# Moving one w2 row between partition halves, starting two programs on a new fetch block, and shortening the VectorE program in a decode kernel

## The chip, the cores and the metric

The kernel runs on one core of one Trainium2 chip. The time is the device time of that core in microseconds (us). The medians here come from 3 to 9 runs, and an interval is a 95% interval over fast runs. The core's executions agree within about 0.15%. The span on a profile page (399.3 us before) is about 1.3 us shorter than the timed run it belongs to (400.63 us).

Words used below. A *DMA engine* is one of the 16 that the page counts for the core. A *completion* is one engine's count on a load's semaphore: a 128-partition load has 16 of them here, and the trace has the time of each. A DMA of 8 partitions has eight. The eight engines on which these run are called *lower*, the other eight *upper*. The recorded texts write 0-7 or "the eight lowest" for the lower and 8-15 for the upper ones. These numbers are labels only: no trace numbers the engines.

## The reference

One token of attention with a cache (32 query heads, 4 key/value heads, 65,536 positions, head size 128) plus a small MLP, on the same normalised input:

```python
x  = A_x                                   # [1, 1, 1024], bf16
xn = layernorm(x)
out = x + A(xn, k_cache, v_cache, wq, wo) + B(xn, w1, w2, w3, w4)

def B(x, w1, w2, w3, w4):                  # w1, w2 1024x1024; w3 1024x3584; w4 3584x1024
    h  = gelu(layernorm(x) @ w1)
    hs = concatenate(shifted quarters of h) @ w2   # one position: every shifted quarter is zero
    x1 = x + hs
    return x1 + gelu(layernorm(x1) @ w3) @ w4
```

The caches are 67 MB each, and about 170 MB are read in all. Because there is one position, the vector that meets w2 is zero. The kernel still loads and multiplies w2.

## The kernel before

Everything large goes through three slots of 8 MB in on-chip memory, loaded by 128-partition DMAs from SP. The prologue loads wq, w1 and w2, and w3. The middle alternates K and V blocks. The end loads wo and then w4 in four parts. The parts that matter here, with cuts marked:

```python
# w2: rows 8p .. 8p+7 on partition p (in the trace 128 packets of 16 KiB; each engine takes 4.89 to 4.92 us)
kv_load(1, "w1", rows_src(B_w1, 0, 8), 8 * D, b_w1)
_dma(q_sp, chan("w2"), lambda e: e.dma_start(out=KV[:, 1, 8 * D:16 * D], in_=rows_src(B_w2, 0, 8)), writes=b_w2)
kv_load(2, "s2", rows_src(B_w3, 0, 8), 8 * F)
# ... cut ...
for h in range(HKV):                       # 16 small mask products
    for we in range(4):
        _op(q_dve, ... tensor_tensor(out=Yall[:, h, we, :, :], ...))
# ... cut: per group of the softmax, but for the first of a head ...
_op(q_dve, ... tensor_tensor(out=dd[:, k:k + 1], in0=brun[:, k:k + 1], in1=brun[:, o:o + 1], op=ALU.subtract))
_op(q_act, ... activation(ff[:, k:k + 1], dd[:, k:k + 1], ACTF.Exp))
# ... cut: the end ...
w4_parts = [(0, 17), (17, 7), (24, 3), (27, 1)]      # four loads; the last is 256 KB
# PE multiplies each part as it lands; DVE copies the result; SP stores it
# ... cut: SP and ACT issue their first load ahead of the start barrier ...
heads = {e: next(i for i in code if i.opcode == "Drain" and i.engine == e) for e in (nc.sync.engine, nc.scalar.engine)}
```

## Time and profile before

| | |
|---|---|
| time, median of 3 | 400.3 us (400.18 to 400.79) |
| read from HBM | 169.87 MB |
| instruction fetches in the span | five of 16 KiB, two of 8 KiB |
| last load complete | 396.78 us |

Three lines of the page: each engine's busy time, the DMA engines' busy tenths in 40 slices, and the shares by engine of the chain of work that ended last.

```profile
PE 177.8 (45%) x1539; PEld 61.1 (15%) x1539; DVE 221.3 (55%) x260; ACT 23.9 (6%) x50; POOL 7.7 (2%) x31
...
DMA  9999899999999999999999999999999999999995
...
DMA 58%; DVE 25%; PE 14%; issue 1%; ACT 1%; SPq 1%; POOL 0%
```

No compute engine is near full. The DMA engines are busy 90% or more in every slice but the fifth (80% or more) and the last. The 25% of DVE in the chain is not time lost: it is mostly the transposes of line 460 (17%), behind which SP issues a later load. A load issued late does no harm here while the queue ahead of it is still full: the K load issued at 71.52 us stands behind one that completes at 86.92 to 89.22.

The DMA queues (packets, MB, share of 16 engines' time), from the same page:

```profile
q1 hardware_dynamic: 3608, 169.87, 98.7%
q8 instruction: 5, 0.08, 0.1%
q10 hardware_dynamic: 144, 0.00, 0.0%
q14 instruction: 2, 0.02, 0.0%
```

Queue 1 is the kernel's loads. Queues 8 and 14 fetch the engines' programs (the page's kind "instruction"). They are under a thousandth of the bytes (0.10 of 169.97 MB).

The end of the chain, in order of time (start, length, what):

```profile
363.85 32.93 DMA KV<-in_B_w_dram
396.78 0.04 issue
396.82 0.31 PE S_ps L566 x4
397.13 0.02 issue
397.16 0.42 DVE orow L647
```

The kernel ends when the last w4 load is complete on its slowest DMA engine (396.78), plus a fixed tail of about 2.5 us. The 16 completions of this load, read from the semaphore's records in the trace:

```
394.48 394.58 394.65 394.67 394.70 394.71 394.74 394.77 394.85 394.93 394.98
396.08 396.16 396.46 396.51 396.78
```

Eleven engines are done within 0.5 us, and five come 1.1 to 1.8 us after the eleventh. The trace's packets show why. A full 64 KiB packet takes 2.418 us. After a 16 KiB fetch (at 46.4, 81.6, 103.9 and 142.3 us) one engine has a gap of about 1.0 us and then a packet slower by 0.5 us, about 1.55 us together, each time another engine. After the 8 KiB fetches (55.0 and 259.3 us) one engine loses 0.31 + 0.66 = 0.97 us, both times the same one. What an engine has lost it does not regain. The engine that ends the w3 load last (50.48 us) is 2.17 us behind the fifth of that load, and at the end the last is 2.08 us behind the fifth (396.78 against 394.70). In the first load the next packet of an engine starts 2 ns after the last one ends (95 of the 96 packets that start between 4 and 18 us), which leaves nothing to catch up in. That this holds for the later loads too would explain it, and fits the full slices. The fifth 16 KiB fetch, at 394.38 us, adds no late engine: the same number, five, is late in the loads before it.

The groups of instructions that write `Yall` and `dd` (line, engine, operation, count: ns min/median/max, first and last start):

```profile
L395 DVE TENSOR_TENSOR Yall<-M_ps,KV x16: 191/191/191, 36.0 to 39.4; 128x32 bf16<-128x32 f32 x16
...
L500 DVE TENSOR_TENSOR dd<-brun x12: 158/159/160, 95.1 to 364.9; 128x1 f32<-128x1 f32 x12
```

### The profile page before, as it was taken

Reading aid. Unit: us, or ns where it says so; the run is one execution under the profiler, and the core shown is the slowest. Engines: PE = TensorE matmul, PEld = TensorE weight load, DVE = VectorE, ACT = ScalarE, POOL = GpSimd, SP = SyncE. Lnnn points to the kernel's source line nnn. Section 1 sums busy time; section 2 is a strip of 40 time slices with the busy share of each in tenths; the row PEclk is TensorE's granted clock in tenths of the full one; section 3 lists DMA queues with packets and bytes.
Section 4 is the critical chain, followed back from the end, with each engine's and each line's share of the span. In section 5 each row is a group of like instructions: output and inputs, shape, how many; then the busy total and the mean of one; then the engine's idle time right before and its main releaser. Section 6 shows DMA issues by size and latency. Waiting matters only on the chain.

```text
span 399.3 us, 3500 instructions
## 1 busy us (share of the span) xinstructions
PE 177.8 (45%) x1539; PEld 61.1 (15%) x1539; DVE 221.3 (55%) x260; ACT 23.9 (6%) x50; POOL 7.7 (2%) x31
## 2 busy tenths in 40 slices
PE   0035669147134713560358036413661462147394
PEld 0022435012001110110012001100120110012232
DVE  0024230995298539843984597269647952895201
ACT  1000000011001100110011002000100110011000
POOL 5000000000000000000000000000000000000000
PEclk9998656555755665585557555855565558555979
DMA  9999899999999999999999999999999999999995
GB/s 420 420 387 487 382 441 479 440 415 427 415 427 427 433 474 433 420 427 420 433 427 433 473 433 420 421 420 433 433 433 473 433 420 420 420 433 433 416 424 219
DMA packets 3759, 169.97 MB, mean 426 GB/s; under 512 B 548, under 2 KB 552, under 8 KB 808
## 3 DMA queue, kind: packets, MB, share of 16 engines
q1 hardware_dynamic: 3608, 169.87, 98.7%
q8 instruction: 5, 0.08, 0.1%
q10 hardware_dynamic: 144, 0.00, 0.0%
q14 instruction: 2, 0.02, 0.0%
HBM read 169.87 MB, written 0.00 MB: 425 GB/s over the span
## 4 chain that ended last, share of the span: by engine, by line
DMA 58%; DVE 25%; PE 14%; issue 1%; ACT 1%; SPq 1%; POOL 0%
DMA KV<-in_A_k_cache_dram 44%; DVE KV L460 17%; DMA KV<-in_B_w_dram 8%; DMA KV<-in_A_x_dram 6%; PE S_ps L411 3%; PE OT_ps L518 3%; DVE mrow L481 2%; PE M_ps L426 2%; PE S_ps L474 2%; PE S_ps L379 2%; ACT p_sb L496 1%; DVE Yall L395 1%; PE PT_ps L505 1%; DVE pT_f L509 1%; DVE pT_f L419 1%
## 5 line engine op out<-in xcount | busy, mean ns | idle before, releaser
L460 DVE STREAM_TRANSPOSE KV<-KV 128x4096 f32<-128x4096 f32 x32 | 140.3, 4421 | 42.2 <-DMA KV<-in_A_k_cache_dram 42.2
L474 PE MATMUL S_ps<-KV,Ycur 128*32 128x512 bf16 x512 | 60.7, 623 | 126.1 <-DVE KV L460 126.1
L518 PE MATMUL OT_ps<-KV,pT_f 128*32 128x512 bf16 x512 | 46.6, 504 | 1.2 <-DVE pT_f L509 1.2
L474 PEld LDWEIGHTS S_ps<-KV,Ycur 128*32 128x32 bf16 x512 | 14.3, 126 | 158.1 <-DVE KV L460 140.5
L496 ACT ACTIVATE p_sb<-S_ps,brun 128x1024 bf16<-128x1024 f32 x16 | 17.8, 1114 | 274.7 <-DVE brun L494 174.3
L509 DVE STREAM_TRANSPOSE pT_f<-PT_ps 128x512 f32<-128x512 f32 x32 | 22.4, 701 | 14.0 <-PE PT_ps L505 14.0
L481 DVE TENSOR_REDUCE mrow<-S_ps 128x1 f32<-128x1024 f32 x16 | 19.3, 1204 | 11.3 <-PE S_ps L474 11.3
L484 PE MATMUL M_ps<-Rm,Lmat 128*128 128x16 bf16 x16 | 3.1, 194 | 38.0 <-DVE Rm L482 38.0
L505 PE MATMUL PT_ps<-p_sb,permR 128*128 128x512 bf16 x32 | 18.3, 573 | 0.8
L529 DVE SCALAR_TENSOR_TENSOR O_acc<-O_acc,ff,OT_ps 128x512 f32<-128x512 f32 x12 | 9.0, 747 | 14.4 <-PE OT_ps L518 14.4
L518 PEld LDWEIGHTS OT_ps<-KV,pT_f 128*32 128x32 bf16 x512 | 12.9, 114 | 23.6 <-issue 15.5
L411 PE MATMUL S_ps<-KV 128*32 128x512 bf16 x88 | 12.5, 571 | 2.7 <-DVE KV L359 2.7
L339 DVE CAST KV<-KV 128x8 f32<-128x8 bf16 x1 | 0.2, 172 | 22.4 <-DMA KV<-in_A_x_dram 22.4
L578 PE MATMUL S_ps<-KV,o_bf 128*1 128x512 bf16 x64 | 9.7, 476 | 4.8 <-DMA KV<-in_A_wo_dram 4.8
L484 PEld LDWEIGHTS M_ps<-Rm,Lmat 128*128 128x128 bf16 x16 | 1.7, 104 | 49.3 <-DVE Rm L482 49.3
L426 PE MATMUL M_ps<-ident_f,pT_f 64*128 64x2 f32 (+2 forms) x32 | 7.9, 372 | 2.4 <-DVE pT_f L419 2.4
L582 DVE COPY pT_f<-S_ps 1x512 f32<-1x512 f32 x1 | 0.7, 679 | 14.4 <-PE S_ps L578 14.4
L426 PEld LDWEIGHTS M_ps<-ident_f,pT_f 64*128 64x128 f32 (+2 forms) x32 | 7.7, 326 | 4.7 <-DVE pT_f L419 3.4
L419 DVE COPY pT_f<-S_ps 64x512 f32<-64x512 f32 (+1 forms) x3 | 2.1, 685 | 11.3 <-PE S_ps L411 11.3
L505 PEld LDWEIGHTS PT_ps<-p_sb,permR 128*128 128x128 bf16 x32 | 3.3, 102 | 27.2 <-ACT p_sb L496 14.7
L364 PE MATMUL M_ps<-KV 8*128 8x8 bf16 x1 | 0.2, 182 | 16.2 <-DVE Dmat_f L363 16.2
L379 PE MATMUL S_ps<-KV 128*32 128x512 bf16 x64 | 6.5, 593 | 1.4 <-DVE KV L359 1.4
(88 smaller groups left out, 88.8 us busy)
## 6 DMA issues: line engine op xcount, KB each, us to landing
KV<-in_B_w_dram SPq DMA_DIRECT2D x1, 7168.0 KB, 48.4
KV<-in_B_w_dram SPq DMA_DIRECT2D x1, 4352.0 KB, 27.4
KV<-in_B_w_dram SPq DMA_DIRECT2D x2, 2048.0 KB, 28.4
KV<-in_B_w_dram SPq DMA_DIRECT2D x1, 1792.0 KB, 31.4
KV<-in_B_w_dram SPq DMA_DIRECT2D x1, 768.0 KB, 32.8
KV<-in_B_w_dram SPq DMA_DIRECT2D x1, 256.0 KB, 32.9
KV<-in_A_k_cache_dram SPq DMA_DIRECT2D x8, 46.5
KV<-in_A_v_cache_dram SPq DMA_DIRECT2D x8, 28.0
```

Source lines behind the costliest of these rows:

```text
L379: fns.append(lambda e, j=j, b=b, jj=jj: e.matmul(S_ps[32 * jj:32 * jj + 32, b, :], xn_bf[:, j:j + 1].broadcast_to([P, 32]), KV[:, 0, j * H ...
L411: fns.append(lambda e, j=j, k=k, mv=mv: e.matmul(S_ps[32 * (k % 4):32 * (k % 4) + 32, bank + k // 4, :], vec[:, j:j + 1].broadcast_to([P, ...
L426: fns.append(lambda e, b=b, nb=nb, c=c: e.matmul(M_ps[:, c0 + 16 * b + c:c0 + 16 * b + 4 * nb:4], pT_f[0:32 * nb, b, c:512:4], ident_f[0:3 ...
L460: _op(q_dve, lambda e: e.transpose(out=KV32[:, s, o:o + 4096], in_=KV32[:, s, o:o + 4096]), reads=[b_KV[s][sub]], writes=[b_KV[s][sub]], l ...
L474: fns.append(lambda e, we=we, cm=cm, mv=mv: e.matmul(S_ps[32 * cm:32 * cm + 32, n % 4, :], Ycur[:, we, :, :].rearrange("p a g -> p (a g)") ...
L481: _op(q_dve, lambda e: e.reduce_max(mrow[:, k:k + 1], S_ps[:, 2 * k:2 * k + 2, :].rearrange("p b c -> p (b c)"), axis=AX.X), reads=b_S[2 * ...
L496: _op(q_act, lambda e: e.activation(p_sb[:, :, :].rearrange("p b c -> p (b c)"), S_ps[:, 2 * k:2 * k + 2, :].rearrange("p b c -> p (b c)") ...
L505: _op(q_pe, lambda e: e.matmul(PT_ps[:, :], permR[:, :], p_sb[:, n % 2, :], start=True, stop=True), reads=[b_p[n % 2], b_const], writes=[b ...
L509: _op(q_dve, lambda e: e.transpose(out=pT_f[:, n % 2, :], in_=PT_ps[:, :]), reads=[b_PT], writes=[b_pT[n % 2]], loop=True)
L518: fns.append(lambda e, q=q, q4=q4: e.matmul(OT_ps[32 * q4:32 * q4 + 32, g % 2, :], pT_bf[:, n % 2, q, :, 1], KV[:, s, 8192 * sub + 512 * q ...
L529: _op(q_dve, lambda e: e.scalar_tensor_tensor(out=O_acc[:, 0:512], in0=O_acc[:, 0:512], scalar=ff[:, k:k + 1], in1=OT_ps[:, k, :], op0=ALU ...
L578: _grp(q_pe, [lambda e, j=j, jj=jj: e.matmul(S_ps[32 * jj:32 * jj + 1, 1, :], o_bf[:, j:j + 1], KV[:, 0, j * D + 512 * jj:j * D + 512 * (j ...
```

## The change

Its intent, as I read it from its code: let the engines that end early carry more of w2, save instruction fetches by starting PE's and VectorE's programs on a block boundary, and shorten the VectorE program. The diff, cut to its core:

```diff
-_dma(q_sp, chan("w2"), lambda e: e.dma_start(out=KV[:, 1, 8 * D:16 * D], in_=rows_src(B_w2, 0, 8)), writes=b_w2)
+NLO = 2
+NALL = KT_D - NLO // 2                    # seven rows on every partition ...
+_dma(q_sp, chan("w2"), lambda e: e.dma_start(out=KV[:, 1, 8 * D:(8 + NALL) * D], in_=B_w2[0:P * NALL, :]...), writes=b_w2)
+for i in range(8):                        # ... and two more on partitions 0-63, by 8 DMAs of 8 partitions
+    hf, c = divmod(i, 4)
+    p0 = 32 * hf + c
+    _dma(q_sp, chan("w2%d" % i), lambda e, ...: e.dma_start(out=KV[p0:32 * (p0 // 32) + 32:4, 1, ...], in_=src), writes=[b_w2x[i]])
 ...
-for h in range(HKV):
-    for we in range(4):                   # 16 products of 32 columns
+for we in range(4):                       # 4 products of 128 columns
 ...
-_op(q_dve, ... tensor_tensor(out=dd[:, k:k + 1], in0=brun[:, k:k + 1], in1=brun[:, o:o + 1], op=ALU.subtract))
-_op(q_act, ... activation(ff[:, k:k + 1], dd[:, k:k + 1], ACTF.Exp))
+_op(q_act, ... activation(ff[:, k:k + 1], brun[:, o:o + 1], ACTF.Exp, bias=brun[:, k:k + 1], scale=-1.0))
 ...
+for eng, slots in ((nc.tensor, 256), (nc.vector, 128)):
+    eng.addr_align(slots, offset=0, max_nops=0)   # in the trace: a new branch on each, at 0.31 us (PE) and 0.09 us (VectorE)
+    # ... moved in front of the engine's first instruction
```

The w2 product gets two more matmuls, on the two extra rows of partitions 0-63 alone (also in the diff; cut here).

More of the change, by code (lines that the diff above doesn't have):

```diff
@@ L205, in bass_parallel_sum__gqa_block_cached__mixer_s_mlp__decode_kernel @@
         brun = sb("brun", [P, 2], F32)
-        dd = sb("dd", [P, 2], F32)
         ff = sb("ff", [P, 2], F32)
@@ L254, in bass_parallel_sum__gqa_block_cached__mixer_s_mlp__decode_kernel @@
         qT_bf = early(HQ, BF)
-        g_bf = early(KT_D, BF)
+        g_bf = early(2 * KT_D, BF)
         h1g_bf = early(KT_D, BF)
@@ L285, in bass_parallel_sum__gqa_block_cached__mixer_s_mlp__decode_kernel @@
         b_p = [_B(), _B()]; b_pT = [_B(), _B()]
-        b_mrow = [_B(), _B()]; b_R = [_B(), _B()]; b_B = [_B(), _B()]; b_brun = [_B(), _B()]; b_dd = [_B(), _B()]; b_ff = [_B(), _B()]; b_lp = [_B(), _B()]
+        b_mrow = [_B(), _B()]; b_R = [_B(), _B()]; b_B = [_B(), _B()]; b_brun = [_B(), _B()]; b_ff = [_B(), _B()]; b_lp = [_B(), _B()]
         b_Oacc = _B(); b_L = _B(); b_cb = _B(); b_cbW = _B(); b_Mc = _B(); b_o = _B(); b_orow = _B()
@@ L299, in bass_parallel_sum__gqa_block_cached__mixer_s_mlp__decode_kernel @@
         kv_load(1, "w1", rows_src(B_w1, 0, 8), 8 * D, b_w1)
-        _dma(q_sp, chan("w2"), lambda e: e.dma_start(out=KV[:, 1, 8 * D:16 * D], in_=rows_src(B_w2, 0, 8)), writes=b_w2)
+        NLO = 2
+        NALL = KT_D - NLO // 2
+        b_w2x = [_B() for _ in range(8)]
+        _dma(q_sp, chan("w2"), lambda e: e.dma_start(out=KV[:, 1, 8 * D:(8 + NALL) * D], in_=B_w2[0:P * NALL, :].rearrange("(p r) n -> p (r n)", p=P)), writes=b_w2)
+        for i in range(8):
+            hf, c = divmod(i, 4)
+            p0 = 32 * hf + c
+            src = bass.AP(B_w2.tensor, B_w2.offset + (P * NALL + p0 * NLO) * D, [[4 * NLO * D, 8], [1, NLO * D]])
+            _dma(q_sp, chan("w2%d" % i), lambda e, p0=p0, src=src: e.dma_start(out=KV[p0:32 * (p0 // 32) + 32:4, 1, (8 + NALL) * D:(8 + NALL + NLO) * D], in_=src), writes=[b_w2x[i]])
         kv_load(2, "s2", rows_src(B_w3, 0, 8), 8 * F)
@@ L392, in bass_parallel_sum__gqa_block_cached__mixer_s_mlp__decode_kernel @@
                     for we in range(4)], reads=[b_qT, b_const], writes=[b_M])
-        for h in range(HKV):
-            for we in range(4):
-                _op(q_dve, lambda e, h=h, we=we: e.tensor_tensor(out=Yall[:, h, we, :, :],
-                                                                 in0=M_ps[:, 128 + 32 * we + 8 * h:128 + 32 * we + 8 * h + 8].unsqueeze(1).broadcast_to([P, 4, G]),
-                                                                 in1=maskA, op=ALU.mult),
-                    reads=[b_M, b_const], writes=[b_Y], partial=(h + we > 0))
+        for we in range(4):
+            _op(q_dve, lambda e, we=we: e.tensor_tensor(out=Yall[:, :, we, :, :],
+                                                        in0=M_ps[:, 128 + 32 * we:128 + 32 * we + HQ].rearrange("p (h g) -> p h g", g=G).unsqueeze(2).broadcast_to([P, HKV, 4, G]),
+                                                        in1=maskA.unsqueeze(1).broadcast_to([P, HKV, 4, G]), op=ALU.mult),
+                reads=[b_M, b_const], writes=[b_Y], partial=(we > 0))
         _op(q_dve, lambda e: e.tensor_tensor(out=acc[:], in0=xT, in1=xn, op=ALU.add), reads=[b_xT, b_xn], writes=[b_acc])
@@ L402, in bass_parallel_sum__gqa_block_cached__mixer_s_mlp__decode_kernel, with proj @@
         kvstep = KV[:].ap[0][0]
-        def proj(s, o, ncol, vec, bank, reads, c0):
+        def proj(s, o, ncol, vec, bank, reads, c0, nlow=0):
             nper = ncol // P
@@ L407, in proj @@
             fns = []
-            for j in range(KT_D):
+            njs = KT_D + nlow // 2
+            for j in range(njs):
+                pp = P if j < njs - nlow else P // 2
                 for k in range(nt):
-                    mv = bass.AP(KV[:].tensor, s * SLOT + o + j * ncol + 4 * k, [[kvstep, P], [nper, P], [1, 4]])
-                    fns.append(lambda e, j=j, k=k, mv=mv: e.matmul(
-                        S_ps[32 * (k % 4):32 * (k % 4) + 32, bank + k // 4, :], vec[:, j:j + 1].broadcast_to([P, 32]), mv,
-                        start=(j == 0), stop=(j == KT_D - 1), tile_position=(0, 32 * (k % 4))))
+                    mv = bass.AP(KV[:].tensor, s * SLOT + o + j * ncol + 4 * k, [[kvstep, pp], [nper, P], [1, 4]])
+                    fns.append(lambda e, j=j, k=k, mv=mv, pp=pp: e.matmul(
+                        S_ps[32 * (k % 4):32 * (k % 4) + 32, bank + k // 4, :], vec[0:pp, j:j + 1].broadcast_to([pp, 32]), mv,
+                        start=(j == 0), stop=(j == njs - 1), tile_position=(0, 32 * (k % 4))))
             nbank = (nt + 3) // 4
@@ L442, in bass_parallel_sum__gqa_block_cached__mixer_s_mlp__decode_kernel @@
         gelu(M_ps[:, 256:256 + KT_D], KT_D, h1g_bf, b_M, b_h1)
-        proj(1, 8 * D, D, g_bf, 3, b_w2 + [b_const], 272)
+        proj(1, 8 * D, D, g_bf, 3, b_w2 + b_w2x + [b_const], 272, NLO)
         _op(q_dve, lambda e: e.tensor_tensor(out=x1, in0=xn, in1=M_ps[:, 272:272 + KT_D], op=ALU.add), reads=[b_xn, b_M], writes=[b_x1])
@@ L499, in EXP @@
             if not first:
-                _op(q_dve, lambda e: e.tensor_tensor(out=dd[:, k:k + 1], in0=brun[:, k:k + 1], in1=brun[:, o:o + 1], op=ALU.subtract),
-                    reads=[b_brun[o], b_brun[k]], writes=[b_dd[k]])
-                _op(q_act, lambda e: e.activation(ff[:, k:k + 1], dd[:, k:k + 1], ACTF.Exp), reads=[b_dd[k]], writes=[b_ff[k]])
+                _op(q_act, lambda e: e.activation(ff[:, k:k + 1], brun[:, o:o + 1], ACTF.Exp, bias=brun[:, k:k + 1], scale=-1.0), reads=[b_brun[o], b_brun[k]], writes=[b_ff[k]])
         def PT(n):
@@ L651, in bass_parallel_sum__gqa_block_cached__mixer_s_mlp__decode_kernel @@
         code = nc.m.functions[0].blocks[0].instructions
-        heads = {e: next(i for i in code if i.opcode == "Drain" and i.engine == e) for e in (nc.sync.engine, nc.scalar.engine)}
+        heads = {e: next(i for i in code if i.opcode == "Drain" and i.engine == e) for e in (nc.sync.engine, nc.scalar.engine, nc.tensor.engine, nc.vector.engine)}
+        for eng, slots in ((nc.tensor, 256), (nc.vector, 128)):
+            eng.addr_align(slots, offset=0, max_nops=0)
+            align = code[-1]
+            assert align.engine == eng.engine
+            code.remove(align)
+            code.insert(code.index(heads[eng.engine]), align)
         n_before = len(code)
```

## The prediction

> **What bounds the kernel.** The DMA engines. The page's slices show DMA at 9 tenths everywhere, 169.97 MB at 426 GB/s, and the chain of waits gives DMA 58%. A full 64 KiB packet takes 2.418 us in the trace, so one of 16 engines needs about 391.7 us for its share of 10.6 MB (estimate from those two); the span is 399.3. The compute engines have slack: DVE is busy 55%, PE 45%, and every load is issued 15 us or more before the queue ahead of it runs dry (DMA issues: the K load issued at 71.5 us follows one that lands at 87-89). So removed VectorE and prologue work is worth about nothing by itself.
>
> What ends last: the 16 engines' completions of the last w4 load. Eleven come at 394.48-394.98 us, five at 396.08-396.78; then 0.3 us PE, 0.4 us DVE, 1.6 us output DMA. The five late engines were delayed by instruction fetches: the DMA queue view lists "instruction" packets, five of 16 KiB (46, 82, 104, 142, 394 us) and two of 8 KiB (55, 259 us). Each of the first four is followed by a gap of about 1.0 us and a 0.55 us slower packet on one engine, each time another one: about 1.55 us. The two 8 KiB ones cost about 0.97 us each, on the same fifth engine. [...]
>
> **What the change does.**
> 1. w2: [...] Nine rows against seven moves 16 KiB per engine: 0.60 us (2.418/4) from each upper to each lower engine. It helps only if the late engines are the upper ones; the trace doesn't number engines, so this is inferred from the change's intent. Eight small DMAs add perhaps 0.03-0.05 us each on the lower engines (estimate from what is left of the 393 us after the packets), 8 issues of about 0.4-0.7 us on SP and 8 waits of 51 ns on PE, all in slack.
> 2. Alignment and fewer VectorE instructions (12 mask products and 14 subtractions, of 271): the VectorE program fits two 128-instruction blocks, so of its fetches at 55 and 259 us one remains, near 160 us: 0.97 us less on one engine. PE still crosses about as many blocks, so I expect three to five 16 KiB fetches at shifted times, still about 1.5 us each on different engines. Both programs jump at the start; what that fetches falls at about time zero, and could cost one engine another 1.5 us.
> 3. 26 VectorE operations of about 0.16-0.2 us: about 5 us of busy time, off the path.
>
> **Sum.** Late upper engines end at about 396.8 - 0.6 = 396.2; lower engines at about 395.0 + 0.6 + 0.3 = 395.9. The tail is unchanged. Gain about 0.6 us: 399.7 us, 80% range 398.9 to 400.5. Faster by over 2%: 0.005; within 2%: 0.985; slower by over 2%: 0.01.
>
> **What would show it.** The last load's completions in a tighter band: earliest about 395, last about 396.1. VectorE instruction packets 2 to 1 in the span; PE ones 5 to 4-5. DVE busy about 216 us. Same HBM bytes.
>
> **What would make it wrong.** Late engines in the lower half (then 0.6 us slower). A PE fetch near the end, or two PE fetches on one engine (about 1.5 us more). More gain (over 1 us) if alignment takes PE fetches out of the loading time or spreads them. A start-up delay from the jumps, if the timer includes it.

The sum: 396.8 - 0.6 = 396.2 us for the late upper engines, 395.0 + 0.6 + 0.3 = 395.9 us for the lower ones, and so a gain of 0.6 us and 399.7 us. The 0.6 is a quarter of the 2.418 us of a 64 KiB packet.

## The result, and the profile after

401.21 us (401.12 to 401.32, 6 runs) against 400.39 us (400.18 to 400.79, 6 runs of before): slower by 0.8 us. The ratio is 1.0019, interval [1.0006, 1.0032]. Every ratio in this document is the mean time of one kernel's fast runs over that of the other's fast runs of the same rounds, so not quite the ratio of the quoted medians. By the 2% measure this is "the same". It is a loss all the same, because the ranges don't touch, and the prediction had a gain.

The lines of the page after that answer to those above:

```profile
PE 176.2 (44%) x1541; PEld 60.2 (15%) x1541; DVE 217.6 (54%) x236; ACT 25.0 (6%) x50; POOL 7.6 (2%) x31
...
q1 hardware_dynamic: 3736, 169.87, 98.6%
q8 instruction: 6, 0.10, 0.1%
...
q14 instruction: 2, 0.02, 0.0%
```

VectorE has 24 operations fewer and is busy 3.7 us less (foreseen: 26 and about 5 us). But there are six 16 KiB fetches instead of five, and still two of 8 KiB: no fetch was saved. The trace has them at these times:

```
             16 KiB (PE)                                  8 KiB (VectorE)
before        46.38  81.64 103.85 142.25 394.38           55.04 259.28
after   4.53  50.76  83.61 122.38 377.76 393.68     4.29 182.67
```

That these queues belong to PE and VectorE is itself read from the runs: below, aligning one program alone adds packets to one queue alone.

The end of the chain after:

```profile
364.24 33.11 DMA KV<-in_B_w_dram
397.35 0.04 issue
397.39 0.31 PE S_ps L572 x4
397.70 0.02 issue
397.73 0.42 DVE orow L653
```

The last load is complete 0.57 us later (397.35 against 396.78), the tail is as long as before, and the span grew by as much (399.9 against 399.3). Its completions:

```
394.08 394.09 394.15 394.25 394.25
395.10 395.22 395.24 395.30 395.31 395.60 395.64 395.65
396.66 397.29 397.35
```

The aim was a narrower band. It became wider: from 2.30 us to 3.27 us between the first and the last. Two windows at the end show the same for each kernel. The columns are: stretch in us, its length, busy us (and count) of the engines, granted clock, DMA share, GB/s. First before:

```profile
394.00:395.00 1.00, 0.69 (x28) 0.57 (x28) 0.00 (x0) 0.00 (x0) 0.00 (x0) 1.00 0.54 201
396.00:397.00 1.00, 0.68 (x16) 0.28 (x16) 0.00 (x0) 0.00 (x0) 0.00 (x0) 1.00 0.02 8
```

Then after:

```profile
394.00:395.00 1.00, 0.13 (x8) 0.12 (x12) 0.00 (x0) 0.00 (x0) 0.00 (x0) 1.00 0.57 223
396.00:397.00 1.00, 0.26 (x12) 0.20 (x12) 0.00 (x0) 0.00 (x0) 0.00 (x0) 1.00 0.09 35
```

From 396 to 397 us the last engines still move 35 GB/s where before 8 GB/s were left, while the others have nothing left to do.

### The profile page after: what moved, and what is told of

It is laid out like the page before. It is cut to its first block, busy times and chain, and to the rows that moved or that the text cites. A ratio compares the mean times of both kernels' runs of the same rounds, so it can differ in the third digit from the quotient of the medians.

```text
span 399.9 us, 3498 instructions
## 1 busy us (share of the span) xinstructions
PE 176.2 (44%) x1541; PEld 60.2 (15%) x1541; DVE 217.6 (54%) x236; ACT 25.0 (6%) x50; POOL 7.6 (2%) x31
## 4 chain that ended last, share of the span: by engine, by line
DMA 59%; DVE 25%; PE 13%; issue 1%; ACT 1%; SPq 1%; POOL 0%; DVEq 0%
DMA KV<-in_A_k_cache_dram 45%; DVE KV L468 17%; DMA KV<-in_B_w_dram 8%; DMA KV<-in_A_x_dram 6%; PE S_ps L419 3%; PE OT_ps L524 2%; DVE mrow L489 2%; PE M_ps L434 2%; PE S_ps L482 2%; PE S_ps L386 1%; ACT p_sb L504 1%; DVE pT_f L515 1%; PE PT_ps L511 1%; DVE pT_f L427 1%; POOL KV L362 0%
## 5 line engine op out<-in xcount | busy, mean ns | idle before, releaser
L419 PE MATMUL S_ps<-KV 128*32 128x512 bf16 (+1 forms) x90 | 12.4, 530 | 2.7 <-DVE KV L366 2.7
```

The lines of the kernel that those rows point to most:

```text
L419: fns.append(lambda e, j=j, k=k, mv=mv, pp=pp: e.matmul(S_ps[32 * (k % 4):32 * (k % 4) + 32, bank + k // 4, :], vec[0:pp, j:j + 1].broadca ...
```

## The experiments

Two theories to begin with. **A**: the five late engines of the kernel before are all upper ones, as the change's intent supposes. Then the split is good, and the alignment, which fetches two blocks more at the start, spoilt it. **B**: late engines lie in the lower half too. Then the split itself puts 0.6 us onto the engines that end last.

Tiny loads of 8, 4, 2 and 1 rows, the *markers* below, are queued behind the last load to tell the engines apart. The traces show of such loads: a DMA of 8 partitions has eight completions as its data land, and a ninth record just after its issue (in the kernel after, the first DMA of the extra rows has 3.28 us, then 30.80 to 33.05). All eight DMAs of the extra rows complete there in one pattern, about 0.2 us apart. The first has six engines at 30.80 to 30.99, one at 32.00 and one at 33.05, and the second six at 31.01 to 31.19, one at 32.19 and one at 33.25. So they run on the same eight engines. That the 8-row marker runs on these eight, and each smaller marker on some of the engines of the larger one, is read from the completions in the two runs with markers. Which partitions an engine writes in a 128-partition load no trace shows.

| kernel | time, us | before, us | ratio, interval | last load complete | 16 / 8 KiB fetches |
|---|---|---|---|---|---|
| after | 401.21 | 400.39 | 1.0019 [1.0006, 1.0032] | 397.35 | 6 / 2 |
| split alone | 401.13 | 400.37 | 1.0021 [1.0007, 1.0035] | 397.37 | 5 / 2 |
| alignment alone | 401.43 | 400.37 | 1.0026 [1.0013, 1.0040] | 397.63 | 6 / 3 |
| split and fewer operations | 401.12 | 400.37 | 1.0017 [1.0004, 1.0031] | 397.43 | 5 / 2 |
| alignment and fewer operations | 400.67 | 400.43 | 1.0005 [0.9992, 1.0019] | 396.80 | 6 / 2 |
| PE aligned alone | 400.49 | 400.43 | 1.0002 [0.9989, 1.0016] | 396.61 | 6 / 2 |
| VectorE aligned alone | 401.53 | 400.43 | 1.0026 [1.0012, 1.0039] | 397.95 | 5 / 3 |
| fewer operations alone | 400.47 | 400.50 | 0.9999 [0.9986, 1.0013] | 396.68 | 5 / 2 |
| split turned over | 402.42 | 400.43 | 1.0049 [1.0036, 1.0063] | 398.90 | 5 / 2 |
| split doubled | 401.83 | 400.46 | 1.0034 [1.0020, 1.0048] | 398.08 | 5 / 2 |
| row on two engines | 402.71 | 400.46 | 1.0056 [1.0042, 1.0070] | 398.94 | 5 / 2 |

All gave correct results. Every kernel of the table but the kernel after (6 runs) had 5 rounds. The two runs with markers, below, are single ones.

### Which engines are late

```diff
                     w4_dma(i)
+                for kk in (8, 4, 2, 1):
+                    _dma(q_sp, chan("mk%d" % kk), lambda e, kk=kk: e.dma_start(out=mark[0:kk, ...64 columns], in_=A_k_cache[0, 0, 0:kk, 0:64]), ...)
```

> The kernel before, plus four tiny marker DMAs (8, 4, 2 and 1 rows of 128 bytes) queued behind the last w4 load. [...] Theory A [...]: all eight completions of the 8-row marker lie within 0.5 us, near 394.6-395.1 us. Theory B (the late engines are mixed): at least one completion of the 8-row marker comes 1.3 us or more after the others, at 396 us or later. Time as before, within 0.5 us.

One run, 400.55 us (state unknown, as for any single run; before 400.37). The markers' completions, without the record made at issue:

```
8 rows   394.77 394.80 394.84 394.87 394.98   396.43 396.45 396.80
4 rows   394.97 395.02 395.16                 396.98
2 rows   395.19 395.34
1 row    395.51
```

Each smaller marker's completions lie 0.17 to 0.18 us behind some of the next larger one's (396.98 behind 396.80, 395.19 and 395.34 behind 395.02 and 395.16, 395.51 behind 395.34). Three of the eight lower engines are late, and the last of all (396.62 for the load in this run, 396.80 for the marker behind it) is among them. The two engines of the 2-row marker are in time, and of the four of the 4-row marker one is late (396.98): it is the last of all, and the trace shows that the 8 KiB fetches delay it (0.98 us behind the fifth engine in the loads before the fetch at 259 us, 1.95 us after it). So theory A's premise is false. That run had the load's late completions at 396.22 to 396.62, six of them: three lower, and so three upper.

The same markers in the kernel after:

> The kernel after with the four marker DMAs behind the last load. Theory: three completions of the 8-row marker are late, at 396.7-397.6, and five come at 395.2-395.6; all that come before 394.5 and those near 395.6 belong to engines 8-15. Rival: the last completions of the load (397.3) are not among the 8-row marker's.

One run, 401.17 us. The 8-row marker came at 395.46, 395.54, 395.60, 395.66, 395.76 and 397.25, 397.44, 397.50. The last three of the load (397.05, 397.26, 397.30) are therefore lower engines. The five that finish before 394.5 and three of those near 395.6 are upper. The five in time came up to 0.2 us later than I had put them. None of the marker's eight comes near the five that finish before 394.5 (its first is at 395.46). That is as it should be if the marker runs on the engines that carry the extra rows.

### The parts one by one

The split alone. Its diff is the first hunk of the change.

> The kernel before with the w2 split alone. Theory A (all late engines in the upper half; the split itself is good and alignment spoilt it): last completion of the last load near 396.2 us, 0.6 us faster than before. Theory B (a late engine in the lower half, which gets 0.6 us more): last completion at 397.0-397.4, 0.3 to 0.7 us slower than before, that is most of the measured loss comes from the split alone.

401.13 us against 400.37, with the last completion at 397.37. Theory B: this is the whole loss, from the split alone. The end of its chain:

```profile
397.37 0.04 issue
397.42 0.31 PE S_ps L576 x4
```

The upper engines in time now end from 393.90 on and the lower ones at about 395.2, but the late lower ones at 396.67, 396.89 and 397.37.

The alignment alone (the last hunk of the change, with its line for the two engines' first instructions).

> The kernel before with both alignments and nothing else. Theory A (alignment is what lost the time: its jump at the start fetches two more blocks while the loads run): one more 16 KiB and one more 8 KiB instruction packet than before, two of them at 4-5 us, and 0.5 to 1.0 us slower than before. Theory B (the split is what lost it): the same start-up packets, but the last completion within 0.2 us of before's 396.8 and no slower than 0.2 us.

401.43 us: slower too, by 1.06 us, just above the range of theory A. So both theories had a part in it, and the parts don't add: 0.76 and 1.06 us alone, 0.82 us for the whole change. The queues show what happened here:

```profile
q8 instruction: 6, 0.10, 0.1%
...
q14 instruction: 3, 0.02, 0.0%
```

One 16 KiB fetch at 4.23 us and one 8 KiB fetch at 4.31 us are new, and the 8 KiB ones are three: 4.3, 143 and 338 us. The last load's completions end with 396.11, 396.23, 396.29, 396.49, 396.60 and, alone by 1 us, 397.63 (2.94 us behind the fifth engine).

Both parts but the alignment:

```diff
-for eng, slots in ((nc.tensor, 256), (nc.vector, 128)):
-    eng.addr_align(slots, offset=0, max_nops=0)
-    ...
```

> The kernel after without the alignment: split and fewer VectorE operations. It should be as the run with the split alone, within 0.2 us, whichever theory holds, because 26 fewer VectorE instructions do not take away a fetch (the program still crosses the same two block boundaries): two 8 KiB instruction packets. Theory A: 0.6 us faster than before. Theory B: 0.3 to 0.7 us slower.

401.12 us, the same as the split alone (401.13), as expected. The shorter VectorE program unaligned still has two fetches (at 60.8 and 291.7 us).

### What the alignment does

The alignment splits into three questions.

> The kernel after with w2 even again (eight rows everywhere): alignment and fewer VectorE operations alone. Theory (the split is the whole loss, because the last engines are of the lower half): the late lower engines, 397.35 in the kernel after, come 0.6 us earlier; upper ones 0.6 later, to 396.25; last completion about 396.75, time 400.2 to 400.6, the same as before. Rival (the start-up fetches of the alignment cost it by themselves): 401.0 or more.

> The kernel before with only PE's program aligned. One more 16 KiB packet than before, near 4 us. Theory (what counts is the sum of fetches on one engine, and PE's fetches go to different engines): last completion 396.5-396.9, time 400.2 to 400.6, no slower than before. Rival (a start-up fetch costs more than others): 401 or more.

> The kernel before with only VectorE's program aligned, its operations not made fewer. Theory (three 8 KiB fetches instead of two, all on one DMA engine, 0.97 us each): three 8 KiB packets, near 4, 143 and 338 us, last completion about 397.6, alone by 0.9 us or more ahead of the next; time 401.2 to 401.6, as slow as with both alignments. Rival (the jump's own cost, or PE's): 400.4 to 400.8.

The edits: e4 is the kernel after with the w2 hunk taken back. The other two are the kernel before with

```diff
+for eng, slots in ((nc.tensor, 256),):      # PE alone; or ((nc.vector, 128),): VectorE alone
+    eng.addr_align(slots, offset=0, max_nops=0)
```

VectorE aligned alone: 401.53 us, a loss of 1.10 us. PE aligned alone: 400.49 against 400.43, no difference. Alignment with fewer operations: 400.67 against 400.43, an interval that holds 1, just above the range expected. The queues of PE alone, then of VectorE alone:

```profile
q8 instruction: 6, 0.10, 0.1%
...
q14 instruction: 2, 0.02, 0.0%
```

```profile
q8 instruction: 5, 0.08, 0.1%
...
q14 instruction: 3, 0.02, 0.0%
```

So within the span queue 8 is PE's and queue 14 VectorE's. (Before the span's start queue 14 has six more 8 KiB packets in every run; the pages do not count them.) An extra fetch of PE costs the kernel nothing here: six engines are late instead of five (396.06 to 396.61), none later than the last one of before. A third fetch of VectorE delays the same engine a third time: the completions end with 396.37 and then 397.95, one engine 1.58 us behind the next. Three times 0.97 us over the 394.5 to 395.0 of an undisturbed engine gives 397.4 to 397.9.

Why did aligning not save a fetch? Count the VectorE instructions that the trace shows before each 8 KiB fetch:

```
                        fetches, us (instructions before it)     in all
before                         55.0 (51)  259.3 (190)             271
VectorE aligned alone   4.7 (3) 143.6 (120) 338.2 (241)           272
after                   4.3 (3) 182.7 (126)                       252
```

Unaligned, the first fetch in the span comes some 50 instructions into the program; that the program begins inside a block already there is my reading of it. Aligned, it fetches at once, and then again when nearly 128 and nearly 256 instructions are done (120 and 241, or 126). The `addr_align` call took 128 instructions for a block. With 272 instructions that is three fetches. With 252 it is two, as many as before. So the fewer operations pay back what the alignment costs, and no more. For PE it is the same: a fetch at the start is new, the first of before (at 46.4 us, after 211 instructions) moves only to 50.8 us (after 266), and none falls away.

The last part by itself, the second and third hunks of the change:

> The kernel before with the fewer VectorE operations alone, w2 even and nothing aligned. Theory (VectorE has slack everywhere and its shorter program still crosses two block boundaries): two 8 KiB instruction packets, VectorE busy about 4 us less, time within 0.2 us of before. Rival (the removed operations lie on the path): 0.5 us or more faster.

400.47 against 400.50: nothing, with VectorE busy 217.6 us instead of 221.3.

### The split by dose, and turned over

```diff
-NLO = 2
+NLO = 4          # ten rows on partitions 0-63, six on 64-127
```

> The kernel before with twice the split: ten w2 rows on partitions 0-63, six on 64-127. Theory (the last engine is of the lower half and pays 16 KiB, 0.60 us, for each row of difference): last completion about 397.95, time 1.3 to 1.5 us over before, 401.7 to 401.9. Rival (the cost is of the eight small DMAs themselves, their issue or waits, and not of the bytes): as with the single split, 401.0 to 401.3.

401.83 us, 1.37 us over before, with the last completion at 398.08, 1.30 us later than before. The single split gave 0.76 us and 0.59 us. The same eight DMAs with twice the bytes cost about twice as much, so it is the bytes on the lower engines and not the DMAs' issue. The packets of the extra rows agree: all 64 take 0.159 us at 4 KiB in the single split, and about twice that, 0.309 us, at 8 KiB here.

```diff
-p0 = 32 * hf + c
+p0 = 64 + 32 * hf + c       # and the two extra rows' matmuls work on partitions 64-127
```

> The kernel before with the split alone, turned over: nine w2 rows on partitions 64-127 and seven on 0-63, by the same eight DMAs of eight partitions. Theory 1 (an 8-row DMA runs on the eight lowest DMA engines, whatever partitions it writes): those engines still carry 16 KiB more, so as the split to the lower partitions: 401.0 to 401.4 us, last completion 397.2-397.4. Theory 2 (the engine follows the partition written): the lower engines are relieved, the two late upper ones get 0.6 us more: last completion about 396.9, time 400.3 to 400.7.

402.42 us: neither number. The completions of the last load were 395.37 to 395.78 (six), 396.52 to 397.08 (seven), then 398.01, 398.13, 398.90. The *pattern* is theory 1's: two groups as far apart as in the plain split, with the three latest well behind. So the extra bytes still went over eight engines that include late ones, whatever partitions they were written to. But every engine was also about 1.5 us later. This loss arises while the extra rows move. The eight small DMAs completed 0.33 to 0.37 us apart for most of their run, against 0.18 to 0.19 us in the plain split (first data completion of each), and the first completion of the w3 load behind them came at 49.08 us instead of 47.54. The time goes inside the packets and not between them: the 4 KiB packets of the extra rows took 0.311 us at the median (0.159 in the plain split), and the first w3 packet of 56 KiB took 3.34 to 3.58 us on eight engines and 2.27 to 2.73 on the other eight (2.12 on all 16 in the plain split). Why the packets were slower in this run was not shown.

### A try at something better

If late engines lie in both halves, no shift between halves can gain. But the two engines of the 2-row marker were not late (395.19 and 395.34), and that marker had these two completions alone.

```diff
-_dma(q_sp, chan("w2"), ... out=KV[:, 1, 8 * D:16 * D] ...)
+_dma(q_sp, chan("w2"), ... out=KV[:, 1, 8 * D:15 * D] ...)           # seven rows
+_dma(q_sp, chan("w2a"), ... out=KV[48:P, 1, 15 * D:16 * D] ...)      # the eighth on 80 partitions
+for i in range(24):                                                  # and on 48, two by two
+    _dma(q_sp, chan("w2b"), ... out=KV[2 * i:2 * i + 2, 1, 15 * D:16 * D] ...)
```

> The kernel before with the eighth w2 row of 48 partitions loaded by 24 DMAs of two partitions each. The marker run showed that engines 0 and 1 are not late; a 2-row DMA runs on these two alone. So engines 0 and 1 get about 1.55 us more and every other engine 6 KiB (0.23 us) less: last completion about 396.5, time 0.2 us faster than before (400.1 to 400.3), if balance over engines is what bounds it. If the extra DMAs cost more on their engines than their bytes (over 0.03 us each), engines 0 and 1 end last and the time is as before or up to 0.5 us slower.

402.71 us: a miss by over 2 us. Two things went wrong. On their engines the 24 DMAs completed about 0.17 us apart near the end. The packets themselves had become slow: a 2 KiB packet took 0.084 us at the quickest in this run and up to 0.178 near the end. And *all* engines ended later, the first at 395.59 instead of 394.48, though each of the other 14 had fewer bytes (6 KiB by the estimate above, if the 160 KiB of the 80-partition DMA went evenly over 16 engines). Here too packets of w3 were slowed: the first 14 took 2.73 to 3.13 us, against 2.12 in the kernel before. Why was not tested, so it stays open. SP also stalled at the issue, 7.3 us between the 21st (9.28 us) and the 22nd (16.54) of these DMAs. That did not empty the queue: w3 was issued at 20.78 us, and the loads ahead of it ended after 31 us.

No version that I ran beats the kernel before. PE aligned alone and fewer operations alone equal it.

## Why the prediction was wrong

- **What bounds the kernel** (right). The prediction named the 16 DMA engines, five of them late by instruction fetches, with a fixed tail. The split moved the last completion by 0.59 us and the doubled split by 1.30 us, against 0.60 and 1.21 us from the packet time, and the time followed it.
- **Step 1, the split** (wrong, and this is the step that failed). The prediction put "Late upper engines end at about 396.8 - 0.6 = 396.2". It took from the change's intent that the late engines are the upper ones. The markers showed three late engines in the lower half, in their run the last of all among them (396.62). The size, 0.60 us, was right and its sign was not: it was listed under what would make it wrong ("Late engines in the lower half (then 0.6 us slower)"), and the split alone cost 0.76 us of time. It should have been given a chance near even, because nothing in the trace of before spoke for either half. The range 398.9 to 400.5 left no room for it.
- **Step 2, the fetches** (wrong in count, small in effect). "Of its fetches at 55 and 259 us one remains" was false: aligning trades a crossing in the middle for one at the start (4.29 us), and two remain. PE got six 16 KiB fetches, not three to five. I had named the start-up fetches as a risk and then summed as if they were free. On PE they nearly were. On VectorE, a start-up fetch without the shorter program costs 1.1 us, which the fewer operations took back: alignment and fewer operations together lie within the noise of before (1.0005).
- **Step 3, fewer VectorE operations** (right). The trace shows 24 fewer and 3.7 us less busy, where I had written 26 and 5 us, and nothing of it on the path (ratio 0.9999).
- **The sum.** Predicted 399.7, measured 401.21. With the sign of step 1 turned and the rest left, the sum gives about 396.8 + 0.6 = 397.4 for the last completion. Measured: 397.35. That it agrees so closely is partly luck, because the last engine is not the same one in each kernel. Before, it took the PE fetch at 46.4 us. With the split alone it is the one of the 8 KiB fetches (2.52 us behind the first engine before the fetch at 260.2 us, 3.50 after it). In the kernel after it is one that was already 2.27 us behind at the first completed load (23.65 us against 21.38), after the new PE fetch at 4.53 us.

## What to carry to other kernels

This kernel, bound by DMA from start to end, ended 2.5 us after its slowest DMA engine was done (396.78 before, 397.35 after). In a kernel like it, look at all 16 completions of the last load, and count what lands on each engine beside the loads: instruction fetches here cost 1 to 1.5 us each, on one engine. Before moving bytes from "late" to "early" engines, tell the late ones apart by measurement, for instance with tiny DMAs of 8, 4, 2 and 1 rows queued behind the last load. Aligning the two programs saved no fetch here: each got a new one at its start (at 4.53 us on PE, 4.29 us on VectorE), and the span had six 16 KiB fetches instead of five and two of 8 KiB as before.
